# Start-up of a Fourier-mixing and gated-convolution kernel: tables in transfers of 48 partitions, w_in in quarters, odd DFT units first

## The chip, the cores and the metric

The kernel runs on one core of one Trainium2 chip. The metric is the device time of one launch in microseconds (us). Times are medians of several runs, and every run named below was in the fast state. Each experiment has runs of the kernel before on the same chip beside it. A ratio is the mean time of one kernel's fast runs over the mean of the other's in the same rounds, so it is not quite the ratio of the medians quoted; in brackets stands its 95% interval. All kernels below gave correct results.

## The reference, cut to what matters

```python
def reference(x, w_in, conv_w, w_out):       # x: 8 x 3136 x 256 float32
    X = np.fft.fft(np.fft.fft(x, axis=1), axis=2).real.astype(np.float32)
    h = np.maximum(X @ w_in, 0.0)             # d_ff = 1024
    c = conv over 3 rows of h with conv_w     # edges padded with zeros
    return (h / (1 + np.exp(-c)) @ w_out).astype(np.float32)
```

The three weights arrive as float64; x is float32.

## The kernel before

The DFT over the rows is a product with tables of cosines and sines, one for even and one for odd frequencies. Before that product x is folded on VectorE, by adding and subtracting mirrored parts, and the folded x is multiplied with the tables in nine "units" on TensorE: four for odd frequencies, four for even ones, and the feature unit, which supplies one edge row. The DFT over the 256 features is merged into the first matrix product (`blocks`). A float64 weight is made float32 on VectorE, which is called narrowing: seven instructions for each piece.

The main loop has 256 cycles: 8 batches, 4 chunks of rows, 8 blocks of features. Batch b + 1 is folded and transformed during batch b. Only batch 0 has nothing to hide behind, so its fold, its units and the narrowing are the start-up. These parts matter:

```python
def load_tables(par):                    # 0: even, 1: odd
    for i in range(2):                   # 49 rows each
        nc.sync.dma_start(out=to[i:NP:2], in_=dft_seq[0:NP // 2, st, HQ * i:HQ * (i + 1)]...)
    nc.sync.dma_start(out=to[NP:KR], ...)               # a rest of one row
# [...]
load_tables(1)                           # behind x, in the middle of its queue
for i in range(2):                       # w_in in halves
    w_in[i].load(nc.sync)
    if i == 0:
        load_tables(0)
# [...]
for f in fold_ops(0):
    f()
w_out.load(nc.sync)                      # 2 MB
for par in (1, 0):
    mend_tables(par, half)               # ScalarE: waits for each table in turn
for i, u in enumerate(us[j] for j in (0, 1, 4, 2, 3, 5, 6, 7, 8)):
    u.matmuls(0, 1)                      # TensorE
    u.copy()                             # ScalarE
    if i == 2: flip()
    u.fin()                              # VectorE (feature unit: GpSimd)
    if i < 2:
        w_in[0].narrow(i, slice(0, H))   # 512 columns in one instruction
    if i == 1: row()                     # er <- last row of qt, a copy of 6 KB
    if i == 2:
        store()                          # ed <- er, to DRAM
        spread(0, range(len(chunks)))    # eb <- ed, to all partitions, four chunks
        for f in load_ops(1, 0, nc.sync): f()   # x of batch 1
    if i == 6: blocks(0)
# [...]
seed(steps[0])                           # ScalarE: pa <- eb * ge
products(steps[0])                       # TensorE: pa += ...
copies(steps[0])                         # ScalarE: h <- pa
# in cycle t: products(t + 1), combine(t) on VectorE, some narrowing, the rest
```

The edge row goes from `qt` to a row tile `er` (a small copy), gets its sums from GpSimd, goes to DRAM (`ed`), is broadcast to all partitions (`eb`), and seeds the first product `pa`. I call this the edge-row chain. The first combine cannot start without it.

## Time and profile before

| | before |
|---|---|
| first measurement, 3 runs | 1270.16 us (1269.85 to 1271.46) |
| busy share of the span: TensorE, VectorE | near full from the third of 40 slices on |
| odd table used by ScalarE, even table used | 29.34 us, 40.32 us |
| first combine of the main loop (T0) | 62.24 us |

### The profile page before, as it was taken

To read this page: it belongs to the slowest core of one execution; us is meant where nothing else is said; L and a number is where in the kernel's file an instruction comes from. 1 tells how busy PE (TensorE), PEld (TensorE's weight loads), DVE (VectorE), ACT (ScalarE), POOL (GpSimd) and SP (SyncE) were. 2 spreads that over 40 slices of the span, in tenths; PEclk is the share of its full clock that TensorE was granted. 3 is DMA by queue.
4 is the path that set the end of the run, shared out by engine and by line. 5 is a ranking of instruction groups with operands and counts; after the bars stand their busy time and mean duration, and the time that the engine had idled before them with its cause. 6 is when DMAs were issued, how large, how long until landed. Compare 5 with 4: busy or idle time off the path is not lost.

```text
span 1265.7 us, 15557 instructions
## 1 busy us (share of the span) xinstructions
PE 1186.2 (94%) x4878; PEld 891.4 (70%) x4878; DVE 1146.4 (91%) x1739; ACT 885.4 (70%) x1835; POOL 397.9 (31%) x503
## 2 busy tenths in 40 slices
PE   0877999899999999999999999999999999999998
PEld 0545677677677767777677777777777777777776
DVE  6499998999999989899899989998999878899996
ACT  1344667677767767777767777776777778788885
POOL 5202642424333234242523324242322213222222
PEclk9988999999999999999999999999999999999999
DMA  9401321202212003020202103020011001010000
GB/s 238 146 16 30 98 77 45 58 28 75 64 58 68 26 22 95 25 84 26 72 24 64 49 26 91 31 83 1 26 45 33 30 26 38 28 29 30 30 26 30
DMA packets 47178, 66.06 MB, mean 52 GB/s; under 512 B 5684, under 2 KB 35276, under 8 KB 47096
## 3 DMA queue, kind: packets, MB, share of 16 engines
q1 hardware_dynamic: 41668, 51.93, 13.5%
q0 software_dynamic: 5120, 12.85, 3.7%
q8 instruction: 39, 0.64, 0.2%
q10 hardware_dynamic: 308, 0.29, 0.1%
q14 instruction: 43, 0.35, 0.1%
HBM read 39.26 MB, written 25.74 MB: 51 GB/s over the span
## 4 chain that ended last, share of the span: by engine, by line
PE 62%; DVE 23%; issue 5%; DMA 4%; ACT 4%; POOL 1%; SPq 0%; DVEq 0%; ACTq 0%; POOLq 0%
PE po L91 38%; PE pb L91 9%; PE pa L91 8%; DVE g L568 7%; PE pd L91 6%; DVE h L556 3%; DVE g L589 3%; DMA tab<-dft_seq_dram 2%; ACT nb L545 2%; DVE xh L158 1%; DVE xh L169 1%; DVE w L185 1%; ACT g L581 1%; DMA er<-qt 1%; DVE w L186 1%
## 5 line engine op out<-in xcount | busy, mean ns | idle before, releaser
L91 PE MATMUL po<-wout,g 128*128 128x256 f32 x3072 | 715.4, 382 | 32.4 <-DVE g L589 28.7
L91 PEld LDWEIGHTS po<-wout,g 128*128 128x128 f32 x3072 | 579.0, 190 | 194.5 <-DVE g L589 71.5
L568 DVE SCALAR_TENSOR_TENSOR g<-h,cw,g 128x770 f32<-128x770 f32 (+1 forms) x512 | 554.8, 1084 | 10.6 <-ACT g L562 1.5
L588 POOL TENSOR_TENSOR g<-g,h 128x385 f32<-128x385 f32 (+1 forms) x256 | 239.2, 935 | 743.5 <-ACT g L581 528.7
L581 ACT ACTIVATE g<-g 128x385 f32<-128x385 f32 (+2 forms) x512 | 244.5, 528 | 222.2 <-DVE g L568 222.0
L545 ACT ACTIVATE nb<-pb 128x386 f32<-128x386 f32 (+2 forms) x484 | 213.6, 494 | 83.0 <-PE pb L91 81.6
L556 DVE CUSTOM_DVE_ANT_0 h<-pa,nb 128x386 f32<-128x386 f32 (+2 forms) x498 | 258.2, 558 | 1.9 <-ACT h L542 1.9
L562 ACT ACTIVATE g<-h,cw 128x770 f32<-128x770 f32 (+1 forms) x256 | 243.6, 952 | 0.2 <-DVE h L556 0.2
L91 PE MATMUL pb<-qt,G 127*128 127x387 f32 (+2 forms) x512 | 213.9, 498 | 0.8 <-ACT nb L540 0.8
L91 PE MATMUL pa<-pt,G 128*128 128x387 f32 (+2 forms) x512 | 212.1, 495 | 0.9 <-ACT pa L513 0.5
L513 ACT ACTIVATE pa<-eb,ge 128x387 f32<-128x387 f32 (+2 forms) x256 | 154.0, 602 | 1.6 <-DVE h L556 1.6
L589 DVE TENSOR_TENSOR g<-g,h 128x385 f32<-128x385 f32 (+1 forms) x256 | 152.0, 594 | 1.2 <-ACT g L581 1.2
L91 PEld LDWEIGHTS pa<-pt,G 128*128 128x128 f32 x512 | 96.6, 189 | 75.4 <-issue 18.7
L91 PE MATMUL pd<-tab,w 99*128 99x196 f32 (+2 forms) x448 | 117.4, 374 | 0.0
L91 PEld LDWEIGHTS pb<-qt,G 127*128 127x128 f32 x512 | 94.0, 190 | 23.4 <-issue 3.5
L133 POOL DMA_INDIRECT xh<-in_x_dram,idx x64 | 98.1, 1533 | 17.9 <-issue 12.4
L91 PEld LDWEIGHTS pd<-tab,w 99*128 99x128 f32 (+1 forms) x448 | 82.9, 190 | 12.8
L608 ACT COPY os<-po 128x256 f32<-128x256 f32 x196 | 58.1, 397 | 10.4 <-PE po L91 5.8
L158 DVE TENSOR_TENSOR xh<-xh 98x1020 f32<-98x1020 f32 (+1 forms) x32 | 45.5, 1421 | 7.4 <-DMA xh<-in_x_dram,idx 7.4
L91 PE MATMUL po<-tab,w 98*128 98x196 f32 (+4 forms) x64 | 18.2, 442 | 26.6 <-ACT tab L223 23.7
L169 DVE TENSOR_TENSOR xh<-xh 98x1024 f32<-98x1024 f32 (+1 forms) x32 | 40.5, 1266 | 0.1
L91 PEld LDWEIGHTS po<-tab,w 98*128 98x128 f32 (+1 forms) x64 | 13.1, 222 | 30.6 <-issue 26.0
(100 smaller groups left out, 398.2 us busy)
## 6 DMA issues: line engine op xcount, KB each, us to landing
out_dram<-os SPq DMA_DIRECT2D x192, 128.0 KB
xh<-in_x_dram SPq DMA_DIRECT2D x16, 784.0 KB
eb<-ed SPq DMA_DIRECT2D x16, 193.5 KB
tab<-dft_seq_dram SPq DMA_DIRECT2D x4, 601.8 KB
raw<-in_moe_w_in_dram SPq DMA_DIRECT2D x2, 1024.0 KB
raw<-in_moe_w_out_dram SPq DMA_DIRECT2D x1, 2048.0 KB
eb<-ed SPq DMA_DIRECT2D x8, 209.0 KB
eb<-ed SPq DMA_DIRECT2D x8, 193.0 KB
```

What stands on the lines that cost most here:

```text
L91: nc.tensor.matmul(o, l, r, start=start, stop=stop, skip_group_check=True)
L133: nc.gpsimd.indirect_dma_start(out=xh[b, h][0:NP, 7 - m].rearrange("p q d -> p (q d)"), out_offset=None, in_=bass.AP(tensor=x.tensor, offs ...
L158: vt(a[:, :, :, 1:D], a[:, :, :, 1:D], r[:, :, :, D - 1:0:-1], op=ALU.add)
L513: act(pa[s][:, 0:n], eb[b, c], AF.Copy, scale=ge[:, f:f + 1])
L545: act(nb[s][:, i, cols], p[:, cols], AF.Copy, scale=-1.0 if i else 1.0)
L556: nc.vector._custom_dve(TENSOR_ADD_SAT, out=to, in0=a[:, cols], in1=c[:, i, cols], s0=BIG, s1=0.0)
L562: act(gs[s], hs[s][:, 0:n], AF.Copy, scale=cw[:, 0, s[2]:s[2] + 1])
L568: stt(out=g, in0=h[:, k:k + n], scalar=cw[:, k, f:f + 1], in1=g, op0=ALU.mult, op1=ALU.add)
L581: act(gs[s][:, c], gs[s][:, c], AF.Sigmoid)
L588: gt(g[:, p], g[:, p], h[:, p], op=ALU.mult)
L589: vt(g[:, v], g[:, v], h[:, v], op=ALU.mult)
L608: nc.scalar.copy(out=osb[:, j % 2], in_=pt[:, j % 2])
```

## The change

Its intent is to shorten the start-up in four ways. (1) The tables travel in transfers of 48 rows, which spread over 16 DMA engines, where 49 rows spread over 7; two rows and one row follow as rests. (2) All of x goes ahead of the tables; a one-element GpSimd copy that reads x holds the tables back. (3) w_in comes in quarters: the first is loaded ahead of x and narrowed ahead of the fold, the others behind the tables. (4) The four odd units go ahead of the even ones, and their first halves run while the second half of x is still being folded. Smaller edits come with these and were not tested by themselves: the feature unit has its own PSUM buffer, the rows of x that are loaded singly are issued from ScalarE's queue, and TensorE forms two products of the DFT matrix with itself that nothing reads (13.34 to 16.8 us). The core of the diff:

```diff
+        m = NP // 2 // 16 * 16
         for i in range(2):
-            nc.sync.dma_start(out=to[i:NP:2], in_=dft_seq[0:NP // 2, st, ...
+            nc.sync.dma_start(out=to[i:2 * m:2], in_=dft_seq[0:m, st, ...
+        nc.sync.dma_start(out=to[2 * m:NP], ...)        # a rest of two rows
@@ loads
+    w_in[0].load(nc.sync)                               # a quarter, ahead of x
+    for h in range(2):
+        for f in load_ops(0, h, nc.sync, nc.scalar):    # all of x
+            f()
-    load_tables(1)
-    for i in range(2):
-        ...
@@ start-up
+    narrow_in(0)
+    blocks(0)
+    ops = fold_ops(0)
+    for f in ops[0:4]:
+        f()
+    nc.gpsimd.tensor_copy(tabs[1][0:1, 0, 0, 0:1], xh[0, 1][0:1, 0, 0, 0:1])
+    for par in (1, 0):
+        load_tables(par)
+    for i in (1, 2, 3):
+        w_in[i].load(nc.sync)
+    for f in ops[4:]:
+        f()
     w_out.load(nc.sync)
-    for i, u in enumerate(us[j] for j in (0, 1, 4, 2, 3, 5, 6, 7, 8)):
+    odds = [us[j] for j in (0, 1, 5, 6)]
+    mirror_tables(0)
+    for u in odds:
+        u.matmuls(0, 2)
+    mend_row(1, half)
+    mirror_tables(2)
+    for i, u in enumerate(odds):
+        u.matmuls(1, 2)
+        u.copy()
+        u.fin()
+        if i == 1:
+            row()
+    narrow_in(1)
+    mend_row(0, half)
+    for i, u in enumerate(us[j] for j in (4, 2, 3, 7, 8)):
         ...                     # store(), spread() and the next x after the feature unit
@@ main loop
     products(steps[0])
     copies(steps[0])
+    blocks(1)                   # blocks(2), blocks(3) and their narrowing in cycles 0 to 3
```

## The prediction

> **What bounds the kernel now.** I read the page's slices first: TensorE is near full from the third slice to the end, VectorE too, and the DMA engines are busy only at the start. So the run is a start-up of about 62 us and then 256 nearly equal cycles. All of the change lies in the start-up and in the first cycles. I therefore asked for the busy time in stretches.
>
> ```profile
> 20.00:25.00 5.00, 0.00 (x0) 0.00 (x0) 1.73 (x4) 0.00 (x0) 0.00 (x0) 1.00 1.00 243
> 25.00:30.00 5.00, 0.00 (x0) 0.00 (x0) 4.90 (x7) 0.66 (x1) 1.47 (x3) 1.00 0.99 249
> ...
> 35.00:40.00 5.00, 5.00 (x10) 2.98 (x10) 0.00 (x0) 0.00 (x0) 0.00 (x0) 1.00 0.44 166
> ```
>
> Columns after the stretch and its length: busy TensorE matmul, weight load, VectorE, ScalarE, GpSimd, then clock, DMA share, GB/s. Up to 30 us all DMA engines are busy; from 35 to 40 us only 0.44 of them are, and VectorE and ScalarE do nothing. The chain that ended last says what they wait for:
>
> ```profile
> 7.17 8.25 DMA xh<-in_x_dram
> 15.45 0.83 SPq L213
> 16.27 0.04 issue
> 16.32 23.92 DMA tab<-dft_seq_dram
> ```
>
> (start, length, what.) The even-parity table is asked for at 15.45 us and has landed at 40.27 us. The timeline shows the two ScalarE operations that wait for the two tables, and the longest VectorE idle time:
>
> ```profile
> 29.34 0.94 ACT L223 ACTIVATE tab<-tab,half 2x786 f32<-2x786 f32 x1 [22.39 <-DMA tab<-dft_seq_dram]
> ...
> 40.32 0.94 ACT L223 ACTIVATE tab<-tab,half 2x786 f32<-2x786 f32 x1 [6.72 <-DMA tab<-dft_seq_dram]
> ...
> 41.64 0.36 DVE L293 TENSOR_TENSOR as<-as,po 128x196 f32<-128x196 f32 x1 [10.59 <-ACT as L289]
> ...
> 62.24 0.56 DVE L556 CUSTOM_DVE_ANT_0 h<-pa,nb 128x385 f32<-128x385 f32 x1 [1.95 <-ACT h L542]
> ```
>
> The odd table lands at 29.3, the even one at 40.3. ScalarE runs in order, so the first `as` copy, whose matmuls were done around 36 us, waits behind the second of these, and VectorE idles 10.59 us. The last line is the first combine of the gated part; call its start T0 = 62.24 us.
>
> What sets the end after T0? The waits of VectorE between 62.5 and 178 us hold nothing but the 1.9 us ahead of this first combine, and the stretch 62.2 to 178.5 has VectorE busy 113.1 of 116.3 us (the rest are gaps of some 20 ns between instructions). So for 116 us VectorE alone sets the pace; after that TensorE catches up and both alternate. TensorE's gaps in that stretch, such as 69.1 to 73.6 us waiting for `w_in` to be narrowed, cost nothing by themselves. The end should follow T0 one for one, as long as VectorE's work after T0 is unchanged and stays without gaps.
>
> **What the Trainium skill says.** "DMA: Bandwidth & Descriptors", section "Why a DMA increments its semaphore by 16 and not by 1": a copy is spread over the largest k up to 16 that divides the slowest dimension of both sides. 49 rows give 7 engines, 48 give 16. The trace agrees: while only tables are moving the share is 0.44, and 7/16 = 0.4375. The rate there was 166 GB/s, so 24 GB/s per engine. The same page, "Issuing engines are not separate DMA queues", says that all issuers share the 16 engines; the trace agrees in that with all engines busy the total was 243 to 249 GB/s whoever issued. "TensorE: Matmul & The Clock Gate", Part 1, "What's actually happening": the array runs at half clock until it has been busy for a window of about 3.4 us, and again after one idle. Here the 392-column passes started 0.65 us apart at 36 us and 0.33 us apart from 47 us on, so the halving is seen; it took about 6 us of work from 33.65 us on to get warm, longer than the page's window.
>
> **The change, part by part.** All later times are estimates from durations in this trace.
>
> *x first.* Ahead of the tables now stand the first quarter of w_in (512 KB), the DFT matrix (256 KB) and all of x (4 x 784 KB): 3.9 MB. In the kernel before, 3.6 MB had arrived by 17 us, at some 245 GB/s, so I expect x complete at 18.5 us, where its last rows came at about 23 us before. A GpSimd copy that reads the second half of x holds the tables back until its plain rows have landed; then about 1.5 us pass from issue to first data, as for the first x load (issued 0.75, data from 2.2 us).
>
> *Tables on 16 engines.* 1.2 MB each. At 245 GB/s a table takes 5.0 us: odd table at about 25 us (29.3 before), even table at about 30 us (40.3 before). The rate could be higher (7 engines ran at 24 GB/s each; 16 of those would be 390).
>
> *First quarter of w_in ahead of the fold.* Narrowing a 128x256 piece takes 7 instructions, 2.65 us in all (65.29 to 67.94 us). Two pieces follow conv_w's at 6.0 us: to 11.3 us. Before, VectorE waited for x until 9.53 and again until 11.35 us, so this costs little. The fold then runs without the 3.23 us hole: half 0 from about 11.7 to 20.5, half 1 to 29.5 us (31.05 before). The odd features of half 0 are there at 16.7, of half 1 at 26 us.
>
> *ScalarE.* The mirror is cut in two: 4 operations of about 0.5 us (before, 4 of 0.892), then two mends of 0.55, then 4 more. From 25: 27.1, 28.2, 30.3 us.
>
> *Odd units.* 16 matmuls, each recorded as two passes: 16 passes of 196 columns (0.33 us cold, 0.17 warm) and 16 of 392 (0.65 cold, 0.33 warm), so 15.7 us cold, 7.9 warm. First halves from 27 us, some 6 us of it cold: to about 34. Second halves warm, 3.9 us: to 38. VectorE's share ends at about 39 us; the row `er` leaves at 37 (47.25 before).
>
> *Second quarter, even units.* Narrowing takes 5.3 us on VectorE, 39 to 44.3. Meanwhile TensorE does the feature unit (0.85 us) and four even units of 1.4 us each, done by 44.6. The even fins are 4 x 0.9 us: to 48 us. The other branch: feature copies 1.3 us, GpSimd sums 3.2 us, then 4.9 us from the store of `er` to the first broadcast landed (52.57 to about 57.5 before): 39 + 1.0 + 3.2 + 4.9, about 48 us. Both branches meet at 48. Before, T0 came 2.16 us after the first `pa` matmul (60.08); so T0 is about 50.2 us, 12.0 earlier.
>
> *After T0.* What VectorE must still narrow is equal: four 128x256 pieces of w_in and eight of w_out. But now only one piece, not two, stands between the first and the second combine, and the blocks of quarter 1 (8 passes of 256 columns and 8 of one column, about 2.6 us warm, 4.5 cold) stand on TensorE ahead of the second step's products (1.95 warm). The second combine can start at about T0 + 4.7 (warm) to 8 (cold); VectorE is through at T0 + 3.2. I put this new hole at 2 us.
>
> Sum: 12.0 - 2 = 10 us, and 1270.16 - 10 = 1260.
>
> **Rivals.** (a) *The bytes decide, not the engines.* If start-up were bound by all bytes at 245 GB/s, 16 engines gain nothing. For it: DMA was full until 30 us. Against it: from 33 to 47 us it was at 7/16. In a milder form, x and tables run at 200 GB/s because tables of 96 partitions collide with other traffic; everything moves 3 to 4 us later, the gain is 6: 1264. (b) *VectorE or ScalarE takes over.* Narrowing two quarters of w_in (10.6 us) ahead of the even fins is now in series, and the mirror and mends sit behind each other on ScalarE. If x were landed by 10 us, the fold would be waiting for narrowing. That is a T0 of 53 to 54, so 1263. (c) *TensorE was the bound in the first cycles after all.* It lost about 13 us between 66 and 80 us waiting for w_in, and the quarters remove this. If the end followed TensorE, the gain would be 10 plus up to 12: 1248. Against it: VectorE had no hole from 62.24 to 178. (d) *The broadcast of `er` is slow* because the x loads of the next batch and w_out share the engines: it took from 52.57 to 59 at worst; T0 moves by 2, 1262.
>
> **Range and chances.** The table rate is worth about -2 to +4 us, the cold clock +-2, the hole after T0 from 0 to 5 us. Together: 1255 to 1264.5. A gain of over 2% needs 25.4 us, i.e. T0 at 37 us, before the odd units can be done: 0.01. A loss of over 2% has no mechanism in the start-up: 0.005. Within 2%: 0.985.
>
> **What would show it right or wrong.** DMA share near 1.00 while only tables move; the mends that wait for tables at about 27 and 37 us, no longer DMA-bound for the second; the 10.59 us hole of VectorE gone, smaller ones (some 4 to 5 us) between the fold and the first odd fin; the first combine at 48 to 53 us; a hole of 0 to 5 us ahead of the second; VectorE then without gaps for over 100 us. The prediction is wrong if the tables still land after 35 us, if x itself comes later than 20 us, or if T0 moves by 12 us and the end does not follow.

## More of the kernel before

From the page of the kernel before, its span and two rows of the slices (busy tenths in 40 equal slices of 31.6 us):

```profile
span 1265.7 us, 15557 instructions
...
DVE  6499998999999989899899989998999878899996
...
DMA  9401321202212003020202103020011001010000
```

VectorE is at 6 and 4 tenths in the first two slices only, where the transfers are also at their busiest. The waits of VectorE in the first 170 us tell what those missing tenths are (what waited, for what; us in total, times, the longest):

```profile
DVE as L293 <- ACT as L289: 10.6, 1, 10.6
DVE xh L158 <- DMA xh<-in_x_dram,idx: 7.4, 3, 3.5
DVE cw L409 <- DMA raw<-in_moe_conv_w_dram: 4.0, 1, 4.0
DVE pt L274 <- issue: 3.4, 1, 3.4
DVE h L556 <- ACT h L542: 1.9, 1, 1.9
```

The largest stands behind a ScalarE copy. That copy waited behind ScalarE's use of the even table, as the prediction shows. The last one is the wait ahead of the first combine. From there to 170 us VectorE waits for nothing.

## The result, and the profile after

| | median | lowest to highest | runs |
|---|---|---|---|
| before | 1270.01 us | 1268.97 to 1271.46 | 4 |
| changed | 1265.70 us | 1264.73 to 1267.16 | 4 |

The ratio is 0.9966 [0.9949, 0.9984]. The gain is about 4.3 us, where 10 were predicted, and the median lies outside the predicted range. A caution for reading the two profiles side by side: the profiled execution of the kernel before (1267.65 us) was faster than each of its timed runs above, and that of the changed kernel (1267.16 us) was the slowest of its four. So the two spans below differ by only 0.5 us.

From the page of the changed kernel, the same rows as before:

```profile
span 1265.2 us, 15611 instructions
...
DVE  7499999999999989899899988998999878899996
...
DMA  7601321212212003020202103120011001010000
```

The first slice of VectorE rose by a tenth, the second did not, and the rest is the same to a tenth here and there. The waits of VectorE up to 170 us, changed kernel:

```profile
DVE h L555 <- ACT h L541: 9.1, 2, 6.4
DVE as L296 <- ACT as L292: 7.4, 1, 7.4
DVE xh L152 <- DMA xh<-in_x_dram,idx: 3.6, 2, 1.9
DVE cw L412 <- DMA raw<-in_moe_conv_w_dram: 3.1, 1, 3.1
```

The wait of 10.6 us became 7.4 us, and the waits for x were halved. But a new group stands at the top: VectorE waits 6.4 us ahead of the first combine, where it had waited 1.9, and 2.8 us more ahead of the second. The timeline gives the moment:

```profile
58.79 0.56 DVE L555 CUSTOM_DVE_ANT_0 h<-pa,nb 128x385 f32<-128x385 f32 x1 [6.35 <-ACT h L541]
```

T0 came 3.45 us earlier than before, not 12. VectorE had been through with its own work at 52.44 us (58.79 less the 6.35 of waiting). The chain of waits of the changed kernel, from the tables to T0 (start, length, what), says what it waited for:

```profile
19.66 1.13 POOL tab L629
20.80 0.75 SPq L210
...
22.71 7.42 DMA tab<-dft_seq_dram
...
30.24 1.91 ACT tab L230 x4
...
32.20 8.19 PE po L91 x22
...
41.57 4.68 DMA er<-qt
...
48.85 1.31 DMA ed<-er
50.17 4.39 DMA eb<-ed
...
54.59 0.59 ACT pa L512
...
55.23 2.94 PE pa L91 x4
```

This is the edge-row chain, and VectorE's narrowing is no longer part of it between the tables and T0. The stretches show the transfers below it (columns as in the prediction: busy TensorE, its loads, VectorE, ScalarE, GpSimd, clock, DMA share, GB/s):

```profile
20.00:22.40 2.40, 0.00 (x0) 0.00 (x0) 2.33 (x4) 0.00 (x0) 1.05 (x2) 1.00 0.11 18
22.40:27.60 5.20, 0.00 (x0) 0.00 (x0) 5.13 (x7) 0.00 (x0) 1.58 (x3) 0.58 1.00 250
27.60:30.00 2.40, 0.03 (x1) 0.06 (x1) 2.37 (x4) 0.00 (x0) 0.76 (x2) 0.50 0.98 173
...
36.00:43.00 7.00, 7.00 (x40) 4.63 (x38) 2.83 (x8) 1.77 (x4) 0.00 (x0) 0.94 1.05 385
...
55.20:58.80 3.60, 3.57 (x6) 2.19 (x7) 0.01 (x1) 1.38 (x3) 0.00 (x0) 0.50 0.98 275
```

From 20.0 to 22.4 us the transfers are nearly idle (share 0.11), because the tables were asked for at 20.80 us. From 22.4 to 27.6 us 16 engines carry tables at 250 GB/s, as predicted. From 36 to 43 us, when the edge row is to leave, weights are moving at 385 GB/s. And in the first products `pa`, from 55.2 us on, the granted clock was 0.50. (The clock column is of use only from the first recorded change on: in the kernel before it says 1.00 from 35 to 40 us, where the passes of 392 columns came 0.65 us apart, twice the 0.33 us of later ones.)

To compare kernels without the luck of one execution I used a number that comes out of every trace: the start of the fifteenth first-combine instruction. It is past all start-up work, at 149.41 us before and 148.66 us after. The span less this number is between 1116.1 and 1116.6 us in 18 of the 20 profiles and 1115.1 us in the other two, although the start itself ranges over 13 us. So the end follows VectorE's start-up one for one. Up to that combine, VectorE's time splits into work and holes (idle times over 0.15 us), and both count.

| start-up of VectorE, us | T0 | second combine | holes | work | fifteenth combine | span |
|---|---|---|---|---|---|---|
| before | 62.24 | 67.86 | 27.9 | 121.5 | 149.41 | 1265.7 |
| changed, first profile | 58.79 | 64.70 | 24.3 | 124.3 | 148.66 | 1265.2 |
| changed, second profile (after_again) | 57.29 | 62.72 | 22.0 | 124.6 | 146.59 | 1262.9 |

The change removed 3.6 to 5.9 us of holes and added 2.8 to 3.1 us of work. The work comes from the pieces: one of 512 columns took 3.78 us before (its seven instructions from 42.19 us on: 0.42 + 3 x 0.43 + 3 x 0.69), and the same data in two pieces of 256 takes 2 x 2.65 = 5.3 us. There were two such pieces before T0, so the sum is 2 x 1.5 = 3.0 us.

### The profile page after: what moved, and what is told of

It is laid out like the page before. It is cut to its first block, busy times and chain, and to the rows that moved or that the text cites. A ratio compares the mean times of both kernels' runs of the same rounds, so it can differ in the third digit from the quotient of the medians.

```text
span 1265.2 us, 15611 instructions
## 1 busy us (share of the span) xinstructions
PE 1190.4 (94%) x4898; PEld 896.7 (71%) x4898; DVE 1148.7 (91%) x1753; ACT 886.5 (70%) x1847; POOL 396.3 (31%) x501
## 4 chain that ended last, share of the span: by engine, by line
PE 62%; DVE 23%; issue 6%; ACT 4%; DMA 3%; POOL 1%; SPq 0%; DVEq 0%; POOLq 0%; ACTq 0%
PE po L91 38%; PE pb L91 9%; PE pa L91 8%; DVE g L567 7%; PE pd L91 6%; DVE h L555 3%; DVE g L588 3%; ACT nb L544 2%; DVE xh L152 1%; DVE xh L163 1%; DVE w L179 1%; ACT g L580 1%; DMA eb<-ed 1%; DMA er<-qt 1%; DVE w L180 1%
## 5 line engine op out<-in xcount | busy, mean ns | idle before, releaser
L91 PE MATMUL po<-wout,g 128*128 128x256 f32 x3072 | 715.1, 382 | 37.2 <-DVE g L588 33.2
L567 DVE SCALAR_TENSOR_TENSOR g<-h,cw,g 128x770 f32<-128x770 f32 (+1 forms) x512 | 554.0, 1082 | 10.6 <-ACT g L561 1.5
L91 PE MATMUL pd<-tab,w 98*128 98x196 f32 (+3 forms) x448 | 117.4, 374 | 0.0
L91 PEld LDWEIGHTS pd<-tab,w 98*128 98x128 f32 (+1 forms) x448 | 82.9, 190 | 12.8
L181 POOL COPY w<-xh 98x4 f32<-98x4 f32 (+1 forms) x32 | 24.5, 765 | 19.6 <-DVE xh L163 14.5
L339 POOL TENSOR_TENSOR er<-as 1x197 f32<-1x197 f32 (+1 forms) x16 | 13.0, 812 | 55.8 <-ACT as L331 29.3
```

Of the source, the lines that this page charges most:

```text
L91: nc.tensor.matmul(o, l, r, start=start, stop=stop, skip_group_check=True)
L567: stt(out=g, in0=h[:, k:k + n], scalar=cw[:, k, f:f + 1], in1=g, op0=ALU.mult, op1=ALU.add)
```

## The experiments

There were five sets on three chips: 1 and 2 on one, 3 and 4 on another, 5 on a third. Sets on one chip share all but one of their runs of the kernel before (the medians in the first column). Each kernel has five or six runs. All outputs are right.

| set, before | kernel | median us | ratio [95%] | T0 | holes | work |
|---|---|---|---|---|---|---|
| 1, 1268.58 | after_again | 1264.84 | 0.9969 [0.9956, 0.9983] | 57.29 | 22.0 | 124.6 |
| | tab48_only | 1261.36 | 0.9945 [0.9932, 0.9959] | 56.15 | 21.8 | 121.4 |
| | blocks_late | 1262.31 | 0.9952 [0.9938, 0.9965] | 56.89 | 19.3 | 124.5 |
| | wout_late | 1265.53 | 0.9972 [0.9958, 0.9986] | 55.15 | 22.8 | 124.7 |
| 2, 1268.6 | after_49 | 1273.34 | 1.0038 [1.0024, 1.0052] | 64.94 | 31.3 | 123.5 |
| | early_trigger | 1262.44 | 0.9953 [0.9940, 0.9965] | 54.81 | 19.1 | 124.6 |
| | row_pool | 1264.38 | 0.9967 [0.9953, 0.9980] | 56.96 | 22.2 | 124.4 |
| | gather_late | 1264.86 | 0.9966 [0.9952, 0.9979] | 57.67 | 22.7 | 124.4 |
| 3, 1269.65 | tab48_pieces | 1266.44 | 0.9969 [0.9955, 0.9983] | 60.85 | 23.3 | 124.6 |
| | tab48_mend | 1260.11 | 0.9920 [0.9907, 0.9934] | 55.05 | 20.9 | 121.1 |
| | row_act | 1263.99 | 0.9949 [0.9936, 0.9963] | 56.84 | 21.1 | 124.6 |
| | early_blocks | 1260.25 | 0.9924 [0.9911, 0.9938] | 54.58 | 16.8 | 124.9 |
| 4, 1269.62 | gather_held | 1265.09 | 0.9960 [0.9947, 0.9974] | 56.77 | 21.7 | 125.3 |
| | wide_pieces | 1265.35 | 0.9962 [0.9949, 0.9974] | 58.28 | 25.6 | 121.8 |
| | all_repairs | 1261.43 | 0.9931 [0.9917, 0.9944] | 55.10 | 21.6 | 121.9 |
| | all_and_row | 1260.78 | 0.9927 [0.9914, 0.9941] | 54.14 | 19.5 | 122.5 |
| 5, 1269.62 | tab48_row | 1260.06 | 0.9925 [0.9912, 0.9939] | 54.50 | 19.8 | 121.5 |
| | early_row | 1262.84 | 0.9946 [0.9934, 0.9959] | 56.26 | 19.1 | 124.3 |

T0, holes and work are of the profiled execution, in us. The kernel before differs by 1.1 us between the sets, so a comparison across sets is uncertain by at least that; there I give the start of the fifteenth combine beside the medians.

### Which part carries the gain

**after_again**: the changed kernel once more, without an edit.

> The changed kernel once more, for the size of the gain and a second sample of its start-up. The two profiles differ by 0.5 us in span, the medians of the runs by 4.3 us. If the profiles are typical (start-up moves 3.45 us, a new hole of VectorE gives 2.8 back), the ratio is 0.999 to 1.000; if the kernel before was profiled in a lucky execution, the ratio is again 0.996 to 0.997 and this profile shows a first combine earlier than 58.8 us or the kernel before one later than 62.2 us.

It repeated the gain: 3.7 us.

**tab48_only**: the kernel before, with nothing but the new table transfers.

```diff
-            nc.sync.dma_start(out=to[i:NP:2], in_=dft_seq[0:NP // 2, ...
+            nc.sync.dma_start(out=to[i:2 * m:2], in_=dft_seq[0:m, ...
+        nc.sync.dma_start(out=to[2 * m:NP], ...)
```

> The kernel before with nothing but the tables in copies of 48 rows (plus 2 rows). Theory 1, engines: the even table lands at 33 to 35 us instead of 40.3, the first combine moves 5 us and the time falls by 4 to 6 us, as much as the whole change brought. Theory 2, bytes: the start-up is bound by what all transfers bring together at 245 GB/s, the even table still lands after 38 us, and the time stays within 1.5 us.

This part alone gained 7.2 us, and was 3.5 us faster than the whole change. Its timeline holds the same two ScalarE lines that the prediction shows of the kernel before:

```profile
23.76 0.95 ACT L228 ACTIVATE tab<-tab,half 2x786 f32<-2x786 f32 x1 [16.81 <-DMA tab<-dft_seq_dram]
...
34.21 0.94 ACT L228 ACTIVATE tab<-tab,half 2x786 f32<-2x786 f32 x1 [6.14 <-DMA tab<-dft_seq_dram]
```

The odd table was used at 23.76 us (29.34 before) and the even one at 34.21 us (40.32 before), 5.6 and 6.1 us earlier, and T0 moved by 6.1 us. The changed kernel, which holds its tables back behind x, used the odd table only at 30.24 us.

**after_49**: the changed kernel, with tables of 49 rows again.

```diff
-            nc.sync.dma_start(out=to[i:2 * m:2], in_=dft_seq[0:m, ...
-        nc.sync.dma_start(out=to[2 * m:NP], ...)
+            nc.sync.dma_start(out=to[i:NP:2], in_=dft_seq[0:NP // 2, ...
```

> The changed kernel with its tables in copies of 49 rows again; all else as changed. Theory 1 (the parts overlap: with the odd units first and the tables behind x, only the odd table is on the path, and it moves alone in both cases, at 170 GB/s on 7 engines or 245 on 16, less a tail on two engines): odd table about 1 to 2 us later, the even table not waited for, time 1 to 2.5 us above the changed kernel. Theory 2 (the parts add: 48 rows are worth some 7 us in any order, and the rest of the change costs 3.5 us): time 6 to 8 us above the changed kernel, slower than the kernel before.

It was 4.7 us slower than the kernel before. So the other three parts, taken together, lose by themselves, and the 48 rows carry the whole gain. How it lost was instructive: the odd table was used at 32.4 us, only some 2 us later than in the changed kernel. The edge row, however, did this:

```profile
44.09 0.73 SPq L343 DMA_DIRECT2D er<-qt  x1
...
53.55 0.90 ACT L347 ACTIVATE er<-er 1x392 f32<-1x392 f32 x1 [6.45 <-DMA er<-qt]
```

It took 9.5 us from issue to use. By then the transfers issued ahead of it ran on a part of the engines only, for 8 us (the last two columns are the DMA share and GB/s):

```profile
44.00:52.00 8.00, 7.50 (x51) 6.06 (x49) 6.33 (x19) 2.34 (x6) 0.00 (x0) 1.00 0.47 174
```

From 52 to 53.5 us the share was 0.11, and then the row was in use. The trace also holds the moments at which each DMA engine reported its part of a transfer as landed (semaphore updates, which no view of `prof` prints). The row came in three parts, at 52.60, 53.09 and 53.53 us; the last engines to report w_out did so at 52.89, 53.35 and 53.54. So the row landed with the last of the weights. This reads as a backlog of tables, w_in and w_out on the engines that the 49 rows load more than the others. The Trainium skill, "DMA: Bandwidth & Descriptors", section "Queues, rings and completion order", says that each DMA engine takes the descriptors of a ring in ring order. A small copy issued late would therefore start behind the large ones issued earlier on the same ring; the 9.5 us agree with that. Ring order alone is not shown to be the cause, though: in row_pool and row_act below the row came from another queue and waited about as long.

### The two ends of the odd chain

**early_trigger**: the one-element copy and the loads behind it stand ahead of the first fold operations, so GpSimd meets the copy before its own fold work.

```diff
-    ops = fold_ops(0)
-    for f in ops[0:4]:
-        f()
     nc.gpsimd.tensor_copy(tabs[1][0:1, 0, 0, 0:1], xh[0, 1][0:1, 0, 0, 0:1])
     # load_tables and w_in[1..3].load
+    ops = fold_ops(0)
+    for f in ops[0:4]:
+        f()
```

> The changed kernel with the small GpSimd copy that releases the tables ahead of the fold's GpSimd copies instead of behind them. Theory 1: the trigger waited for the fold and not for x; tables are asked for at 17 to 18 us instead of 20.8, the odd table lands 2 to 3 us earlier and the first combine and the end move by 2 to 3 us. Theory 2: the tables then share the engines with the last rows of x, the fold's second half comes later by as much, and the time moves less than 1 us.

It gained 2.4 us against after_again. The timeline:

```profile
17.95 0.64 POOL L625 COPY tab<-xh 1x1 f32<-1x1 f32 x1 [5.76 <-DMA xh<-in_x_dram]
...
27.71 1.91 ACT L230 ACTIVATE tab<-tab 99x392 f32<-99x392 f32 x4 [7.63 <-DMA tab<-dft_seq_dram]
```

In the changed kernel the copy ran at 19.66 us, behind two GpSimd operations of the fold, and took 1.13 us; here it ran as soon as x had landed, at 17.95 us. The table was used 1.8 to 2.5 us earlier than in the two profiles of the changed kernel, and T0 2.5 us earlier than in after_again. So the first of the lost microseconds is shown: the hold-back was placed behind other work of its engine.

**blocks_late**: `blocks(1)` behind the products of step 1.

```diff
-    blocks(1)
+    at(0, "act", lambda: blocks(1))
```

> The changed kernel with the blocks of quarter 1 behind the products of the second step instead of ahead of them. Theory 1 (VectorE alone sets the pace after the first combine, and its hole ahead of the second combine is handed on in full): the hole of 2.8 us goes, the time falls by 2 to 3 us below the changed kernel. Theory 2 (the hole is slack, TensorE catches up later): within 0.7 us of the changed kernel.

It gained 2.5 us against after_again, and the second combine came 3.05 us after T0 (56.89 to 59.94 us) instead of 5.43. So the hole ahead of the second combine, which the prediction had put at 2 us, was real, counted, and was not needed.

**early_blocks**: both edits together.

> The changed kernel with both repairs that helped: the tables' trigger ahead of the fold's GpSimd copies (-2.4 us) and the blocks of quarter 1 behind the second step's products (-2.5 us). They touch different holes, so they should add: 1260 us, with holes of about 17 us and 124.5 us of work up to the fifteenth combine. If the second hole only existed because the first combine was late, the sum is under 3 us: 1262.

It reached 1260.25 us, 4.6 us below after_again's median in another set, and its fifteenth combine started 4.9 us earlier (146.59 to 141.65). The two gains, 2.4 and 2.5 us, add. Its waits of VectorE:

```profile
DVE h L555 <- ACT h L541: 5.2, 1, 5.2
DVE as L296 <- ACT as L292: 4.3, 1, 4.3
```

Only one wait ahead of a combine is left. Its holes are the smallest of all kernels, 16.8 us.

### VectorE's extra work

**tab48_pieces**: tab48_only, with w_in's first half narrowed in pieces of 256 columns.

```diff
-            w_in[0].narrow(i, slice(0, H))
+            for j in range(2):
+                w_in[0].narrow(i, slice(j * H // 2, (j + 1) * H // 2))
```

> The kernel before with tables of 48 rows, and the first half of w_in narrowed in pieces 256 wide instead of 512, as the changed kernel does; nothing moved. Theory 1 (the end is VectorE's work plus its holes): VectorE's work up to the fifteenth combine rises from 121.4 to about 124 us, the holes stay near 22 us, and the time is 2 to 3 us above the kernel with 48 rows alone. Theory 2: the longer narrowing fills holes that were there (3.4 us before the even units), and the time stays within 1 us.

It cost 5.1 us against tab48_only by the medians of two sets, and 4.7 us at the fifteenth combine (143.17 to 147.86): work rose by 3.2 us, holes by 1.5.

**wide_pieces**: the changed kernel, with a quarter narrowed in 7 instructions of 2 x 256 columns instead of 14.

```diff
-        for t in range(2):
-            w_in[i].narrow(t, slice(0, N4))
+        w_in[i].narrow(slice(0, 2), slice(0, N4))
```

> The changed kernel with the first two quarters narrowed in 7 instructions of 512 elements each instead of 14 of 256. Theory 1 (work counts in full): VectorE's work up to the fifteenth combine falls from 124.5 to about 122, the time by 1.5 to 2.6 us. Theory 2 (there are holes ahead of the fold and ahead of the first combine that take up the saving): work falls as much, holes rise as much, time within 0.7 us.

It removed 2.8 us of work, the same extra work, and gained nothing: holes rose by 3.6 us against after_again. The pair shows when work of an engine matters. In the old order VectorE's narrowing is itself on the way to T0 (it feeds `blocks(0)`), so the pieces cost their length and more: the chain of waits of tab48_pieces holds them, and that of wide_pieces holds the edge row and no narrowing. In the new order the edge row sets T0, so freed VectorE time turns into waiting.

### The edge row behind the weights

**wout_late**: the 2 MB of w_out loaded after the broadcast.

```diff
-    w_out.load(nc.sync)
@@ behind spread(0, range(len(chunks)))
+            w_out.load(nc.sync)
```

> The changed kernel with the load of w_out behind the broadcast of the edge row, instead of ahead of the row. Theory 1: the row, 6 KB, took 4.7 us to land because it stood behind 2 MB of w_out on the same queue; without it, it lands in about 2 us, the first combine comes 2 to 3 us earlier and the time falls as much. Theory 2: the last-but-one wait is for the even units and the narrowing of quarter 2, which end at 52.4 us; then the first combine moves by less than 1 us.

The row was in use 2.8 us after its issue, and T0 came at 55.15 us, 2.1 earlier than in after_again, but the time did not move. The waits of VectorE show a new one:

```profile
DVE wout L412 <- DMA raw<-in_moe_w_out_dram: 2.9, 1, 2.9
```

The narrowing of w_out waited 2.9 us for its data and gave the gain back.

**row_pool** and **row_act**: the row's copy issued from GpSimd's or ScalarE's queue.

```diff
-            nc.sync.dma_start(out=er[b], in_=PQ[b][1][P - 1:P, :])
+            (nc.sync if b else nc.gpsimd).dma_start(...)     # row_pool
+            eng.dma_start(...)     # row_act: row(nc.scalar), one unit later
```

> The changed kernel with the first batch's edge row copied from GpSimd's queue, so that it does not stand behind w_out on the same queue; w_out stays early. Theory 1: it lands in 2 to 2.5 us instead of 4.7, the first combine comes 2 to 2.5 us earlier, the end moves by about 2 us, and there is no wait for w_out as there was when w_out was put back. Theory 2: the row shares the engines with w_out anyway and lands no earlier; no change.

> The changed kernel with the edge row of the first batch issued from ScalarE's queue. GpSimd's queue brought nothing (4.5 us to land), which can mean that GpSimd's own queue is slow, or that w_out delays the row whatever its queue. If the queue's order delays it: lands in about 2 us, sums start about 2 us earlier than 45.3, the first combine and the end move 1 to 2 us. If sharing the engines with w_out delays it: lands as late as before, no change beyond 0.7 us.

From issue to use the row took 4.5 us by GpSimd's queue and 3.9 us by ScalarE's, against 4.7 and 3.5 us in the two profiles of the changed kernel. The times are within a microsecond of after_again. This agrees with what the skill's "Issuing engines are not separate DMA queues" says, already cited in the prediction: the other queue ends on the same engines. So the order within SyncE's own queue is not what held the row, and the engines are. In the changed kernel 13 engines had reported their part of w_out by 44.14 us and the other three at 44.90, 45.47 and 46.08; the row's three parts came at 44.34, 45.65 and 46.25. In row_act the three slowest parts of w_out came at 43.01, 44.50 and 44.65 us, those of the row at 42.86, 44.69 and 44.83. Twice the row's last parts followed within 0.2 us.

**gather_late** and **gather_held**: the indirect loads of the next x, whose issue occupies GpSimd and whose data shares the engines with the broadcast, moved into cycle 1 or 3.

```diff
-            for f in load_ops(1, 0, nc.sync):
-                f()
+    for fn in load_ops(1, 0, nc.sync):
+        at(1, "load", fn)          # gather_held: at(3, ...)
```

> The changed kernel with the loads of the next batch's x put into the second cycle of the gated part, behind the broadcast of the edge row. Theory 1: the broadcast took 4.4 us from issue because the x rows were ahead of it on the engines; now 2.5 to 3 us, and the first combine and the end move 1 to 2 us. Theory 2: the broadcast is bound by its own 128 small rows; no change beyond 0.7 us.

> The changed kernel with the next batch's x loads on GpSimd behind the second gating product, so that they cannot start before the broadcast has landed. Theory 1 (they share the engines with the broadcast): the broadcast lands 2.5 to 3 us after its issue instead of 3.4 to 4.4, first combine and end 1 to 1.5 us earlier. Theory 2 (the broadcast is slow by itself: 128 rows from one place): under 0.7 us. If x then comes too late for the fold in the sixth cycle, a new hole of VectorE shows near 90 us.

gather_late told nothing: nothing held GpSimd back, and it ran the loads at 48.9 us all the same. In gather_held they did come later; the broadcast then took 3.3 us from its issue to the seed, but the time stayed (1265.09). So the next x is not what made the broadcast slow, for the most part: 3.3 us of it are its own.

**tab48_mend**: tab48_only, with the even table's mend taken out of ScalarE's way, behind the copies of the first two units (odd ones) and ahead of the feature unit.

```diff
-    for par in (1, 0):
-        mend_tables(par, half)
+    mend_tables(1, half)
@@ in the loop over units
+        if i == 2:
+            mend_tables(0, half)
```

> The kernel before with tables of 48 rows, and the mending of the even table behind the first two units' copies on ScalarE. Theory 1: VectorE's hole of 5.1 us after the fold was the first copy standing behind that mend in ScalarE's order, not a lack of data; narrowing now starts at about 31.5 instead of 36.1 us, and 3 to 4.5 us of the hole go to the end: 1257 to 1258.5. Theory 2: the even table's landing (34.2 us) still sets the row and the even units; narrowing early only moves the hole to the end of the start-up, less than 1.5 us gained.

It attacks the wait of VectorE behind the even table directly, still 5.1 us in tab48_only, and gained only 1.25 us by the medians of two sets (1.1 us at the fifteenth combine, 143.17 to 142.05). The row now left at 37.2 us instead of 41.1 us, in the middle of w_out's transfer, and ScalarE's flip had to wait for it. **tab48_row** therefore adds one move, which issues w_out directly behind the row:

> The kernel before with tables of 48 rows, the even table mended later, and the load of w_out directly behind the edge row's. Theory 1 (the row waits for w_out): it lands in 2 us instead of 5.8, the sums start at about 40 instead of 43.1, VectorE's hole of 3.3 us at 41 us goes, and the first combine comes at 51.5 to 53 instead of 55.05; time 1257 to 1258.5. Theory 2 (the row is slow by itself, or the broadcast now stands behind w_out and gives it back): within 1 us of 1260.1.

The flips of the two kernels, tab48_mend and then tab48_row:

```profile
43.00 0.93 ACT L354 ACTIVATE er<-er 1x392 f32<-1x392 f32 x1 [4.82 <-DMA er<-qt]
```

```profile
36.84 0.76 SPq L350 DMA_DIRECT2D er<-qt  x1
...
38.80 0.93 ACT L354 ACTIVATE er<-er 1x392 f32<-1x392 f32 x1 [1.14 <-DMA er<-qt]
```

The row took 2.0 us from issue to use ahead of w_out and 5.8 us behind it (37.2 to 43.0). So the wait behind the weights is shown. It earned nothing here, though: the median is 1260.06 us, the same. The chain of waits of tab48_row, from the even table to the first `pa`, says why:

```profile
15.86 18.46 DMA tab<-dft_seq_dram
...
34.34 0.95 ACT tab L228
...
35.38 7.85 PE po L91 x45
43.23 3.44 PE pa L91 x8
46.67 4.60 PE po L91 x32
...
52.34 1.55 PE pa L91 x4
```

The edge row is not on it, and neither is it on that of tab48_mend. In the old order TensorE works on from the landing of the even table: even units, `blocks(0)`, and the last even units behind it. For those VectorE waited 6.0 us:

```profile
DVE pt L279 <- ACT as L275: 6.5, 2, 6.0
```

The row's store to DRAM, which now stood behind w_out (42.15 us to the broadcast's issue at 45.77), did no harm here.

**early_row** is the same move on early_blocks.

> The changed kernel with early trigger and late blocks, and the load of w_out directly behind the edge row's. Theory 1: row lands in 2 us, sums start at 41 instead of 42.6, first combine 1 to 1.5 us earlier, time 1259. Theory 2: the store of the summed row and its broadcast now stand behind w_out; no change or up to 1 us later.

It was 2.6 us slower than early_blocks by the medians of two sets (1.8 us at the fifteenth combine, 141.65 to 143.45). The row was there within 2.8 us, but the store stood behind w_out from 44.62 to 47.98 us, where it takes 1.31 us in the changed kernel.

**all_repairs** (early_blocks, wide_pieces and gather_held together) and **all_and_row** (row_act as well):

> All repairs: early trigger, blocks of quarter 1 later, next x held, wide pieces. If they add: 2.4 + 2.5 + 1.2 + 2 = 8 us below the changed kernel, about 1257 us, ratio to the kernel before 0.990. If the chain over the edge row (row, sums, store, broadcast) sets the first combine alone, wide pieces bring nothing here: 1259.

> The same with the edge row issued from ScalarE's queue. In the changed kernel this brought 0 to 2 us. If the row is on the path here: 1 to 1.5 us below all_repairs. If w_out delays it whatever its queue, within 0.7 us of it.

They gave 1261.43 and 1260.78 us, no better than early_blocks. VectorE's work fell by 3.0 us in all_repairs, and its holes rose by 4.8. Its chain of waits to T0 runs over the edge row, as that of early_blocks does: the row left at 38.71 us and the seed came at 50.90 (38.33 and 50.38 in early_blocks), so the work that was saved became waiting, as in wide_pieces.

### The best versions

tab48_mend, tab48_row and early_blocks are 9.4 to 9.6 us faster than the kernel before and 4.5 to 5.2 us faster than the changed kernel (by the medians of different sets and by the fifteenth combine), and these runs cannot tell them apart. By effort tab48_mend is the best: a table transfer of 48 rows and one mend moved, and no reordering.

## Why the prediction was right or wrong

**Right.** The end followed VectorE's start-up one for one, in all versions. All transfers of 48 rows ran on 16 engines: the share was 1.00 at 250 GB/s, and 1.2 MB in about 5 us, as worked out. The hole of 10.6 us ahead of the first odd fin shrank, but to 7.4 us and not to the 4 or 5 named. The new hole ahead of the second combine was put at 2 us and was 2.8 and 2.3 us. VectorE went on without gaps after it. The class, within 2%, was right. Of the three signs of being wrong one came, without effect: the last part of the even table landed at 36.95 us (35.88 in the second profile), but nothing waited for it. The odd table was there at 30.13 us, x at 19.1 us, and the end did follow T0. The sign of being right that failed is "the first combine at 48 to 53 us".

**Wrong: the step "so T0 is about 50.2 us, 12.0 earlier".** It was 58.79 us, 8.6 later than predicted. Both branches were to "meet at 48". VectorE's branch was off by 4.4 us (52.44 us), the edge row's by 6.5, and the latter decides. The shape of the chain was right, its terms were not. From the chain of waits shown above:

| term of the edge-row chain, us | predicted | measured | difference |
|---|---|---|---|
| the row `er` leaves | 37 | 41.57 | +4.6 |
| from there until it has landed | 2 | 4.68 | +2.7 |
| flip and sums of GpSimd | 1.0 + 3.2 | 2.60 (46.25 to 48.85) | -1.6 |
| store and broadcast, to the seed | 4.9 | 5.74 (48.85 to 54.59) | +0.8 |
| from the seed to the first `pa` matmul | 0 | 0.64 | +0.6 |
| from there to T0 | 2.16 | 3.56 | +1.4 |
| sum | | | +8.5 |

The first row splits again. The tables were asked for at 20.80 us instead of 18.5 (early_trigger shows this: the hold-back stood behind GpSimd's own work). They landed 9.3 us later, at 30.1 us, instead of 6.5 us later. The large parts were moved at the predicted rate until 27.6 us; then the share stayed at 0.98 but only 173 GB/s moved. By the engines' reports the two large parts had landed at 26.37 and 29.73 us, the rests of two rows and of one row at 29.77 and 30.13 (25.73, 28.18, 29.03 and 29.44 in after_again). So the rests cost 0.4 to 1.3 us. The rest of the tail is open; the even table, issued from 23.44 us on, moved at the same time. From the first half of an odd unit to the row's issue it took 9.4 us (32.20 to 41.57), where 10 were predicted.

The second row is the weights: 2.0 us ahead of w_out, 5.8 us behind it, between tab48_row and tab48_mend. The predicted 2 us came from the kernel before, where the row left at 47.25 us, just when the other transfers ended (DMA share 0.43 until 47 us, 0.02 from 47.5 to 49). What put three engines behind the others is open: the rests of the tables, which two engines each carried, are a candidate that no run varied. The prediction had ordered w_out's load, and looked for its collision only with the broadcast (rival d), not with the row.

The last row is the clock of TensorE. The granted clock was 0.50 in the first `pa` products, and two passes of 386 columns took 1.65 us there, against 0.89 us in the kernel before. Two stretches show when it fell:

```profile
49.00:50.50 1.50, 0.00 (x0) 0.00 (x0) 1.47 (x5) 0.32 (x1) 1.19 (x2) 1.00 0.01 4
50.50:52.50 2.00, 1.62 (x2) 0.50 (x2) 1.94 (x6) 0.00 (x0) 1.70 (x2) 0.51 0.66 175
```

The last even unit ended at 48.98 us and the next matmul started at 50.82; in between, at about 50.5 us, the clock was halved. The wait for the seed (52.44 to 55.23 us) came on top. "TensorE: Matmul & The Clock Gate", cited in the prediction for the odd units, could have told it for `pa` too: the page has the clock halved after an idle window of about 3.4 us, and by the prediction's own numbers TensorE was through with the even units at 44.6 us and met the seed at 48. I applied it to one place of the path and not to the other.

**Right, with a cost that was not named.** What VectorE must still narrow after T0 was equal, as said. Ahead of T0 the prediction had 10.6 us for two quarters (5.3 + 6.2 us measured), but it did not set them against the 7.6 us of the old order: 2.8 to 3.1 us more work, since 256-column pieces replaced 512-column ones. In the changed order it cost little (wide_pieces), because the edge row decided; in the old order it would have cost 4.7 to 5.1 us (tab48_pieces). A slip of the prediction changed nothing: 16 engines at 24 GB/s each are 384 GB/s and not 390.

**The rivals.** (a), slow transfers, was half right: the rate was not lower until 27.6 us, but the odd table came 5 us late. (b), VectorE as the bound, was refuted by wide_pieces. (c), TensorE as the bound of the first cycles, was refuted: with w_in in halves or in quarters, the span less the start of the fifteenth combine stayed the same. (d), the slow broadcast, was right in kind and small (+0.8 us); the slow copy was another one of the same chain.

**What was not foreseen at all** is the division of the gain. The 48 rows alone are worth 7.2 us; the rest of the change, as written, costs 3.5 us on top of them and 4.7 us without them. With the hold-back and `blocks(1)` repaired (early_blocks), it is worth 1.1 us (medians) to 1.5 us (fifteenth combine) beyond the 48 rows, and tab48_mend gets as much by moving one line.

**Open.** The tail of the tables' landing; what puts three engines behind; why tables and x move at about 250 GB/s while w_in and w_out reached 385 (the weights fill 128 partitions and the others 96 to 99, which no run varied); and what the broadcast's own 3.3 us are.

## What to carry to other kernels

When two branches meet, add up both with every copy in them, down to those of a few kilobytes, and ask of each which large transfers were issued ahead of it: the branch with little work and many small copies may be the longer one. Try the smallest part of a change alone before building a new order around it; here one changed row count gave more than the whole. A trigger that holds a transfer back belongs ahead of all other work of its engine.

## What the Trainium skill lacked or had wrong

- "DMA: Bandwidth & Descriptors", section "Why a DMA increments its semaphore by 16 and not by 1": it gives the rule for the number of engines, which held (a share of 0.44 with 49 rows, 1.00 with 48), but no size for the after-effect. After uneven transfers a share of 0.47 lasted for 8 us in after_49, and a later copy of 6 KB landed only at its end, 9.5 us after its issue. In the changed kernel three engines finished w_out 0.8 to 1.9 us after the other 13, and the copy took 4.7 us; with nothing large ahead it took 2.0 us. That it helps nothing to issue the copy from ScalarE (row_act, 3.9 us) fits the section "Queues, rings and completion order", by which a transfer is reported as complete only after every earlier write from that engine, across its queues.
- "TensorE: Matmul & The Clock Gate", Part 1, puts the transition at about 4 us of sustained work, give or take 0.5 us. From the start of the odd units at 32.20 us the changed kernel took about 4.7 us (the granted clock rose between 36.5 and 37 us), the kernel before some 6 us. The page does say that the window runs freely.
- The same page, same part, has the clock halved after an idle window of about 3.4 us. Here it was halved at about 50.5 us, 1.5 us after the last matmul (48.98 us). The page does not say how much idle time within a window is enough.
